# Another order of the sixteen attention units, with the decay table's squares on ScalarE and the first unit's own-key products on GpSimd

## Chip, cores and metric

The kernel runs on one core of a Trainium2 chip. The metric is the device time of one execution in microseconds (us), as the median of several runs; lower is better. Each program was also run once under the hardware profiler, and the rows quoted here come from that execution.

## What is computed

Three blocks follow one another. Cut to what matters:

```python
# attention, batch 4, 8 heads, 768 tokens, head size 48: a decaying state per head
for t in range(S):
    cur = u * k[t] v[t]^T
    y[t] = r[t] (state + cur)
    state = w * state + k[t] v[t]^T
# soft mixture of experts: 3072 tokens x 384, 8 experts with 4 slots each, inner size 1024
logits = x @ phi
d = softmax(logits, over tokens)
slot_input = d.T @ x
slot_out[e] = relu(slot_input[e] @ w1[e]) @ w2[e]
y = softmax(logits, over slots) @ slot_out
# feed-forward: 384 -> 2048 -> 384
out = relu(y @ w_in) ** 2 @ w_out
```

## The kernel before

**Units.** The attention's work is cut into sixteen units, one for each of 4 batches and 4 pairs of heads, in this order. A unit has 768 tokens, taken as six chunks of 128. Its inputs arrive by one group of loads (`load_unit`, L93 and L97) in one of five unit buffers. `decay` (L236, VectorE) multiplies keys and receptances by powers of the decay w from a table. `turns` (L263 to L276) does two transposes on TensorE: the keys of a coming unit, and the attention output of an earlier unit into `xn`, with the copies on ScalarE. `A` (L306) makes the products of keys and receptances inside a chunk, `KV` (L318) the chunk states, `scan` (L322, VectorE) runs the states through the chunks, `cp` (L311, VectorE) copies the masked products, `inter` (L336) and `intra` (L345, copies L348) add up the output: the part from the state and the part inside the chunk. `pr1`, `pr2`, `weigh` and `diag` (L280 to L295) make the term of a token's own key on GpSimd and VectorE. For units 0 to 2 that term is made in another way: `rk` (L491) multiplies keys and receptances elementwise, `dg_of` (L498) sums them on TensorE.

**The decay table.** `base` holds w. L207 to L216 build the table on VectorE: a copy of w, five squares (L209), the reciprocals of all six powers in one instruction (L210), and six products (L216) that double the filled part of the table each time. TensorE meanwhile does warm-up products (`keep_clock`, L227) and fillers (`filler`, L231), whose results nobody reads.

**The soft mixture.** `L` (L371) adds a unit's logits; when the four units of a batch (a block) are through, `soft1a` to `soft1d` take maxima and exponentials, `both` (L408) transposes them, and `soft3` (L463) multiplies them with the block's attention output. That output is `xn`, of which there are two: blocks 0 and 2 use `xn[0]`, blocks 1 and 3 `xn[1]`. `xn[0]` is a part of the big buffer of slot 13 (`sh0`; the names slot_14 in the order's rows are its). `soft4` (L473) adds a block's sums to the totals P2. Of the last block the sums are formed in the lines behind the attention. After it come the experts' first product (`up`, L998) and second (`down`, L1018), the token sums of the experts' output (L1114, with a copy of the middle third on VectorE, L1115), the products of these with w_in (`G`, L1123), and the feed-forward proper, which is TensorE's work to the end (L1166, L1275).

**Loads.** All loads are issued by SyncE (SP) in the order in which they stand in the program, and each waits there until its buffer is free. Besides the units these are the first product's weights w1 in 24 pieces (`load_piece`, L196), the second's, w2, as whole experts (`load_weight` 8 to 15, L193), four quarters of w_in (`load_win`, L149) and sixteen pieces of w_out (`load_wout`, L177). The weights go where a unit's buffer has become free; the first quarter of w_in goes into slot 13, once `xn[0]` has been read for the last time. w_in and w_out hold 8-byte numbers, of which VectorE makes 4-byte ones (L156, L158, L160, three instructions for a piece).

**Order.** The order of instructions on each engine is that of the calls in the program, written out by hand (`tc.manual_schedule()`); the list of calls from `decay(0, 1, EV)` on is what the change rewrites. Each tile's tag and number of buffers sets which earlier use a write waits for.

Of the kernel before, what the change touches and what calls it, by code (L numbers as in the profile page):

```python
# [9 lines left out]
F32R = mybir.dt.float32r  # L10
# [7 lines left out]
def rwkv_softmoe_ffn(ctx: ExitStack, tc: tile.TileContext, un, wt, ph, w1, w2, w_in, w_out, out):  # L18
# [119 lines left out]
    nc.scalar.activation(warm[:, 0:1], warm[:, 1:2], AF.Exp)  # L138
# [90 lines left out]
    def filler(n):  # L229
        for _ in range(n):  # L230
            nc.tensor.matmul(pp[:, 384:512], ident, ident, start=True, stop=True)  # L231

# [250 lines left out]
    keep_clock(6)  # L483
# [62 lines left out]

    decay(0, 1, EV)
    load_piece(10)
    decay(0, 1, OD)
    carry_of()  # L550
    decay(0, 0, EV)
    rk(0, EV)
    decay(0, 0, OD)
    rk(0, OD, nc.vector)
    filler(2)
    turns(None, 0)
    A(0, 0)
    decay(1, 1)
    A(0, 1)
# [3 lines left out]
    filler(2)  # L563
    rsc_of()
    filler(2)
    decay(1, 0)
    filler(2)
    filler(2)
    scan(0)
    cp(0, 1)  # L570
    turns(None, 1)
    ones_of()
    filler(2)
    UT_of()
    diag(0, 0)
    cp(0, 0)
    inter(0)
    rk(1)
    dg_of(1)
    diag(1, 1)  # L580
    intra(0, 0)
    KV(1)
    decay(2, 0)
    decay(2, 1)
    rk(2)
    intra(0, 1)
# [24 lines left out]
    decay(4, 0)
    L(0)
    A(2, 1)
    cp(2, 0)
    inter(2)
    intra(2, 0)
    diag(2, 1)
    cp(2, 1)
    pr2(3)
    decay(4, 1)  # L620
    pr1(4)
    load_piece(5)
    KV(3)
    weigh(3)
    diag(3, 0)
    diag(3, 1)
    scan(3)
    intra(2, 1)
    pr1(5)
    A(3, 0)  # L630
    turns(1, 4)
    decay(5, 1)
    L(1)
    cp(3, 0)
    load_piece(8)
    pr2(4)
    A(3, 1)
    turns(2, 5)
    load_unit(7)
    decay(6, 0)  # L640
    cp(3, 1)
    L(2)
    decay(5, 0)
    A(4, 0)
    inter(3)
    KV(4)
    weigh(4)
    diag(4, 0)
    decay(6, 1)
    scan(4)  # L650
    cp(4, 0)
    load_piece(3)
    intra(3, 0)
    intra(3, 1)
    A(4, 1)
    turns(3, 6)
    L(3)
    soft1d(0)
    pr2(5)
    weigh(5)  # L660
    diag(4, 1)
    A(5, 0)
    cp(4, 1)
    load_piece(15)
    diag(5, 0)
    pr1(6)
    decay(7, 1)
    cp(5, 0)
    pr2(6)
    load_unit(8)  # L670
    soft1a(0)
    soft1b(0)
    load_piece(4)
    inter(4)
    diag(5, 1)
    decay(7, 0)
    KV(5)
    scan(5)
    intra(4, 0)
    intra(4, 1)  # L680
    load_unit(9)
    A(5, 1)
    cp(5, 1)
    turns(4, 7)
    load_piece(17)
    pr1(7)
    weigh(6)
    decay(8, 0)
    both(0)
    c_max(0)  # L690
    A(6, 0)
    inter(5)
    intra(5, 0)
    diag(6, 0)
    cp(6, 0)
    KV(6)
    c_sub(0)
    diag(6, 1)
    load_piece(14)
    pr2(7)  # L700
    intra(5, 1)
    load_unit(10)
    decay(8, 1)
    A(6, 1)
    load_piece(2)
    turns(5, 8)
    load_piece(6)
    pr1(8)
    L(4)
    L(5)  # L710
    cp(6, 1)
    weigh(7)
    scan(6)
    pr1(9)
    soft3(0)
    decay(9, 1)
    diag(7, 0)
    A(7, 0)
    inter(6)
    cp(7, 0)  # L720
    load_piece(23)
    intra(6, 0)
    KV(7)
    intra(6, 1)
    load_unit(11)
    pr2(8)
    scan(7)
    diag(7, 1)
    A(7, 1)
    turns(6, 9)  # L730
    L(6)
    weigh(8)
    A(8, 0)
    diag(8, 0)
    inter(7)
    intra(7, 0)
    cp(7, 1)
    decay(10, 1)
    pr2(9)
    diag(8, 1)  # L740
    soft1c(0)
    KV(8)
    cp(8, 0)
    decay(9, 0)
    scan(8)
    c_exp(0)
    intra(7, 1)
    decay(10, 0)
    c_sum(0)
    A(8, 1)  # L750
    cp(8, 1)
    weigh(9)
    load_piece(16)
    turns(7, 10)
    load_piece(0)
    L(7)
    A(9, 0)
    soft1a(1)
    inter(8)
    soft1b(1)  # L760
    KV(9)
    load_unit(12)
    decay(11, 1)
    load_piece(18)
    intra(8, 0)
    intra(8, 1)
    scan(9)
    KV(10)
    pr1(10)
    pr2(10)  # L770
    load_piece(11)
    diag(9, 0)
    A(9, 1)
    diag(9, 1)
    cp(9, 0)
    load_unit(13)
    turns(8, 11)
    both(1)
    cp(9, 1)
    A(10, 0)  # L780
    inter(9)
    pr1(11)
    weigh(10)
    diag(10, 0)
    intra(9, 0)
    diag(10, 1)
    scan(10)
    KV(11)
    soft1c(1)
    intra(9, 1)  # L790
    A(10, 1)
    c_max(1)
    load_piece(12)
    load_unit(14)
    decay(12, 1)
    load_piece(21)
    cp(10, 0)
    turns(9, 12)
    decay(11, 0)
    pr2(11)  # L800
    L(8)
    pr1(12)
    cp(10, 1)
    L(9)
    A(11, 0)
    scan(11)
    inter(10)
    load_piece(22)
# [540 lines left out]
```

## Time and profile before

| what | value |
|---|---|
| median of 3 runs | 370.85 us (370.64 to 371.09) |
| the profiled execution | 370.69 us, span 369.0 us |
| TensorE products busy | 362.9 us, 98% |
| VectorE busy | 266.8 us, 72% |
| ScalarE busy | 203.6 us, 55% |
| GpSimd busy | 101.8 us, 28% |

The span is the time from the first to the last instruction in the trace. The parts of the kernel lie in it like this: the head to about 16 us, the attention to about 111 us, the experts' first product from 116.5 to 127.7 us, their second from 129.0 to 139.5 us, the first feed-forward product at 141.25 us, and the feed-forward to the end. Busy shares are means over the span; what the rows in the section below show are single stretches.

### The profile page before, as it was taken

To read this page: it belongs to the slowest core of one execution; us is meant where nothing else is said; L and a number is where in the kernel's file an instruction comes from. 1 tells how busy PE (TensorE), PEld (TensorE's weight loads), DVE (VectorE), ACT (ScalarE), POOL (GpSimd) and SP (SyncE) were. 2 spreads that over 40 slices of the span, in tenths; PEclk is the share of its full clock that TensorE was granted. 3 is DMA by queue.
4 is the path that set the end of the run, shared out by engine and by line. 5 is a ranking of instruction groups with operands and counts; after the bars stand their busy time and mean duration, and the time that the engine had idled before them with its cause. 6 is when DMAs were issued, how large, how long until landed. Compare 5 with 4: busy or idle time off the path is not lost.

```text
span 369.0 us, 9048 instructions
## 1 busy us (share of the span) xinstructions
PE 362.9 (98%) x3694; PEld 295.0 (80%) x3694; DVE 266.8 (72%) x457; ACT 203.6 (55%) x441; POOL 101.8 (28%) x119
## 2 busy tenths in 40 slices
PE   7999999999999999999999999999999999999996
PEld 6888888897986637787878888888888888888884
DVE  7879878889675687999876676666666766666663
ACT  3244444544444217987878765555555755555553
POOL 4558886686744112222222400000000000000000
PEclk9999999999999999999999999999999999999999
DMA  7999899999999998333422022000000210000004
GB/s 247 411 366 412 298 376 388 405 376 408 351 360 410 419 417 333 95 110 93 108 92 68 2 85 85 3 0 0 2 1 0 114 60 0 2 1 0 0 2 171
DMA packets 22665, 65.22 MB, mean 177 GB/s; under 512 B 2544, under 2 KB 4832, under 8 KB 22624
## 3 DMA queue, kind: packets, MB, share of 16 engines
q1 hardware_dynamic: 22624, 64.65, 46.5%
q8 instruction: 29, 0.48, 0.5%
q14 instruction: 12, 0.10, 0.1%
HBM read 59.00 MB, written 4.72 MB: 173 GB/s over the span
## 4 chain that ended last, share of the span: by engine, by line
PE 97%; DVE 1%; DMA 1%; ACT 0%; issue 0%
PE ps_A L1275 26%; PE ps_tab L1275 9%; PE ps_kv L1275 9%; PE ps_lg L1275 9%; PE ps_A L306 7%; PE ps_YO L336 3%; PE ps_YE L345 3%; PE ps_YO L1166 3%; PE ps_YE L1166 3%; PE ps_A L998 3%; PE ps_YO L345 3%; PE ps_tab L1018 3%; PE ps_lg L371 2%; PE ps_kv L318 2%; PE ps_YE L269 2%; PE ps_kv L269 1%
## 5 line engine op out<-in xcount | busy, mean ns | idle before, releaser
L1190 DVE TENSOR_TENSOR slot<-slot,slot 128x512 fp32r<-128x512 f32 (+1 forms) x97 | 70.2, 725 | 55.1 <-PE ps_A L1275 18.6
L1275 PE MATMUL ps_A<-slot,slot 128*128 128x512 f32 x429 | 105.1, 389 | 0.0
L1275 PEld LDWEIGHTS ps_A<-slot,slot 128*128 128x128 f32 x429 | 80.5, 188 | 16.7
L1187 ACT CAST slot<-slot 128x512 fp32r<-128x512 f32 x95 | 59.1, 622 | 49.0 <-DVE slot L1184 48.7
L1275 PE MATMUL ps_tab<-slot,slot 128*128 128x512 f32 x144 | 55.5, 392 | 0.0
L1184 DVE TENSOR_TENSOR slot<-slot 128x512 f32<-128x512 f32 x68 | 47.0, 691 | 11.4 <-ACT slot L1177 11.2
L1275 PE MATMUL ps_kv<-slot,slot 128*128 128x512 f32 x144 | 55.1, 389 | 0.0
L1275 PE MATMUL ps_lg<-slot,slot 128*128 128x512 f32 x144 | 55.0, 389 | 0.0
L311 DVE COPY_PREDICATED AT<-mask,ps_A 128x384 f32<-128x384 int32 x63 | 33.5, 584 | 7.6 <-PE ps_A L306 3.2
L1177 ACT ACTIVATE slot<-ps_YO 128x512 f32<-128x512 f32 (+1 forms) x49 | 28.8, 590 | 12.1 <-PE ps_YO L1166 11.5
L1177 ACT ACTIVATE slot<-ps_YE 128x512 f32<-128x512 f32 x48 | 28.8, 599 | 12.1 <-PE ps_YE L1166 11.8
L295 POOL TENSOR_SCALAR_AFFINE_SELECT AT<-dg 128x768 f32<-128x768 f32 x32 | 28.1, 883 | 20.0 <-DVE dg L288 7.4
L1049 POOL TENSOR_TENSOR slot<-wf,slot 128x384 fp32r<-128x384 f32 x16 | 17.3, 1082 | 58.9 <-ACT slot L1044 58.9
L1275 PEld LDWEIGHTS ps_tab<-slot,slot 128*128 128x128 f32 x144 | 27.0, 188 | 6.0 <-issue 0.6
L1275 PEld LDWEIGHTS ps_kv<-slot,slot 128*128 128x128 f32 x144 | 27.0, 188 | 5.7
L1275 PEld LDWEIGHTS ps_lg<-slot,slot 128*128 128x128 f32 x144 | 27.0, 188 | 5.5
L306 PE MATMUL ps_A<-slot 48*128 48x128 f32 x378 | 30.3, 288 | 0.0
L236 DVE TENSOR_TENSOR slot<-slot,ps_tab 112x768 f32<-112x768 f32 (+1 forms) x34 | 29.8, 889 | 0.0
L306 PEld LDWEIGHTS ps_A<-slot 48*128 48x128 f32 x378 | 24.5, 187 | 4.9 <-issue 3.2
L348 ACT COPY xT<-ps_YE 112x384 f32<-112x384 f32 x16 | 7.7, 481 | 23.4 <-PE ps_YE L345 23.4
L284 POOL TENSOR_TENSOR slot<-slot,slot 128x576 f32<-128x576 f32 x13 | 18.5, 1419 | 7.6 <-ACT slot L276 7.5
L1166 PE MATMUL ps_YO<-slot,slot 128*128 128x512 f32 x48 | 18.9, 393 | 0.0
(233 smaller groups left out, 562.0 us busy)
## 6 DMA issues: line engine op xcount, KB each, us to landing
slot<-in_un_dram SPq DMA_DIRECT2D x12, 1344.0 KB, 7.8
slot<-in_w_dram SPq DMA_DIRECT2D x24, 512.0 KB, 9.2
slot<-in_w_dram SPq DMA_DIRECT2D x8, 1536.0 KB, 10.0
slot<-in_w_in_dram SPq DMA_DIRECT2D x4, 1536.0 KB, 10.5
wo<-in_w_out_dram SPq DMA_DIRECT2D x16, 384.0 KB, 3.3
out_dram<-slot SPq DMA_DIRECT2D x18, 256.0 KB, 2.1
slot<-in_un_dram SPq DMA_DIRECT2D x9, 448.0 KB, 6.6
slot<-slot SPq DMA_DIRECT2D x56, 16.0 KB, 1.9
```

Source lines behind the costliest of these rows:

```text
L236: nc.vector.tensor_tensor(x, x, t.unsqueeze(1).to_broadcast(list(x.shape)), ALU.mult)
L284: nc.gpsimd.tensor_tensor(rv, rv, st[n, "kn"] if by is None else by, ALU.mult)
L295: nc.gpsimd.affine_select(out=at, in_=dg.unsqueeze(3).to_broadcast([128, 2, HC, 128]), pattern=[[0, 2], [0, HC], [1, 128]], compare_op=ALU ...
L306: nc.tensor.matmul(p[h][:, i], tv[rows, 1, 2 * i + par], tv[rows, 0, 2 * i + par], start=True, stop=True)
L311: nc.vector.copy_predicated(st[n, "AT", par][:, h], mask.unsqueeze(1).to_broadcast([128, HC, 128]), p)
L345: nc.tensor.matmul(p[o:o + D, i], vv[:, 2 * i + par, h], at[:, h, i], start=False, stop=True, skip_group_check=True)
L1166: nc.tensor.matmul(p, gst[:, 128 * f:128 * (f + 1)], cTall[:, 512 * g:512 * (g + 1)], start=True, stop=True)
L1177: nc.scalar.activation(fs[i, "hr"][:, c], fs[i, "p"][:, c], AF.Relu)
L1184: nc.vector.tensor_mul(gg, hr, hr)
L1187: nc.scalar.copy(part(i, "gh")[:, c], fs[i, "gg"][:, c])
L1190: nc.vector.tensor_tensor(part(i, "gl")[:, c], fs[i, "gg"][:, c], fs[i, "gh"].bitcast(F32)[:, c], ALU.subtract)
L1275: nc.tensor.matmul(o, (hi, lo, hi)[k][:, 128 * j:128 * (j + 1)], (gh, gh, gl)[k], start=(f == 0 and k == 0 and i > 0), stop=(f == NF - 1 a ...
```

## The change

Five things change in the head: the five squares of the table go from VectorE to ScalarE (as activations of the kind Square, with the early exponential of L138 behind them), the copy of w goes to GpSimd, the one reciprocal of all powers becomes three that stand between the products, two of the six warm-up products go, and both halves of unit 0's own-key products are on GpSimd (one half of unit 1's is now on VectorE). A function `idle` is added that nothing calls. Behind that the list of calls is another: the same units in the same order with the same instructions, interleaved in another way, and with the loads at other places between them. Cut to what is spoken of:

```diff
-    nc.scalar.activation(warm[:, 0:1], warm[:, 1:2], AF.Exp)
...
-    nc.vector.tensor_copy(pos[:, 0], base[:, :NP])
     for i in range(5):
-        nc.vector.tensor_mul(pos[:, i + 1], pos[:, i], pos[:, i])
-    nc.vector.reciprocal(neg[:, :6], pos[:, :6])
-    nc.vector.tensor_copy(tabp[:, :, 63:64], neg[:, 0].unsqueeze(2))
+        nc.scalar.activation(pos[:, i + 1], pos[:, i] if i else base[:, :NP], AF.Square)
+    nc.scalar.activation(warm[:, 0:1], warm[:, 1:2], AF.Exp)
+    nc.gpsimd.tensor_copy(pos[:, 0], base[:, :NP])
     for i in range(6):
         n = 1 << i
+        if i == 0:
+            nc.vector.reciprocal(neg[:, 0], base[:, :NP])
+            nc.vector.tensor_copy(tabp[:, :, 63:64], neg[:, 0].unsqueeze(2))
+        elif i in (1, 3):
+            nc.vector.reciprocal(neg[:, i:3 * i // 2 + 2], pos[:, i:3 * i // 2 + 2])
...
-    keep_clock(6)
+    keep_clock(4)
...
-    rk(0, OD, nc.vector)
+    rk(0, OD)
...
-    soft3(2)
-    inter(14)
...
     turns(14, None)
     c_max(2)
     c_sub(2)
+    soft3(2)
+    inter(15)
```

In the rows of the order an engine's instructions stand in sequence; `xN` is a count of like ones in a row. VectorE in the head, before, from the table's first row on; slot_14_84 is slot 13's buffer with the powers of w, ps_tab the table, slot_1_71 unit 0:

```order
L207 COPY slot_14_84<-base 112x4
L209 TENSOR_TENSOR slot_14_84<-slot_14_84 112x4 x5
L210 RECIPROCAL slot_14_84<-slot_14_84 112x24
L211 COPY ps_tab_122<-slot_14_84 112x4
L216 TENSOR_TENSOR ps_tab_122<-ps_tab_122,slot_14_84 112x4x2
...
L236 TENSOR_TENSOR slot_1_71<-slot_1_71,ps_tab_122 112x3x128 x4
L491 TENSOR_TENSOR slot_1_71<-slot_1_71 112x3x128
```

And now:

```order
L213 RECIPROCAL slot_14_84<-base 112x4
L214 COPY ps_tab_121<-slot_14_84 112x4
L219 TENSOR_TENSOR ps_tab_121<-ps_tab_121,slot_14_84 112x4x2
L216 RECIPROCAL slot_14_84<-slot_14_84 112x8
L219 TENSOR_TENSOR ps_tab_121<-ps_tab_121,slot_14_84 112x4x2x2
L219 TENSOR_TENSOR ps_tab_121<-ps_tab_121,slot_14_84 112x4x2x4
L216 RECIPROCAL slot_14_84<-slot_14_84 112x12
...
L244 TENSOR_TENSOR slot_1_71<-slot_1_71,ps_tab_121 112x3x128 x4
L511 TENSOR_TENSOR slot_13_83<-ps_tab_121,slot_14_84 112x512
```

The squares (L209) and the own-key half (L491) are gone from this engine; the reciprocals are three and stand between the products.

TensorE at the end of the attention, before; slot_5_75 is unit 14's buffer, slot_1_71 unit 15's, and L463 reads slot 13's:

```order
L371 MATMUL ps_lg_1867<-xT_1708,phs 32x128 x6
L463 MATMUL ps_A_1876<-slot_14_84,nat_1777 32x385 x6
L336 MATMUL ps_YO_117<-slot_5_75,slot_15_85 48x128 x2
...
L345 MATMUL ps_YE_116<-AT_1790,slot_5_75 48x128 x6
L345 MATMUL ps_YO_117<-AT_1874,slot_5_75 48x128 x6
L318 MATMUL ps_kv_115<-slot_1_71,slot_15_85 48x48 x10
...
L269 MATMUL ps_YE_116<-ident,xT_1909 128x48
...
L371 MATMUL ps_lg_1867<-xT_1808,phs 32x128 x6
L371 MATMUL ps_lg_1867<-xT_1909,phs 32x128 x6
L336 MATMUL ps_YO_117<-slot_1_71,slot_15_85 48x128 x2
```

And now, where L379, L344, L353, L326, L277 and L471 are the lines L371, L336, L345, L318, L269 and L463 of before:

```order
L379 MATMUL ps_lg_1871<-xT_1831,phs 32x128 x6
...
L344 MATMUL ps_YO_116<-slot_5_75,slot_15_85 48x128 x2
...
L326 MATMUL ps_kv_114<-slot_1_71,slot_15_85 48x48 x10
L353 MATMUL ps_YE_115<-AT_1792,slot_5_75 48x128 x6
L353 MATMUL ps_YO_116<-AT_1852,slot_5_75 48x128 x6
...
L277 MATMUL ps_YO_116<-ident,xT_1930 128x48
L471 MATMUL ps_A_1970<-slot_14_84,nat_1799 32x385 x6
L344 MATMUL ps_YO_116<-slot_1_71,slot_15_85 48x128 x2
...
L353 MATMUL ps_YE_115<-AT_1892,slot_1_71 48x128 x6
L353 MATMUL ps_YO_116<-AT_1894,slot_1_71 48x128 x6
L379 MATMUL ps_lg_1871<-xT_1930,phs 32x128 x6
```

The slot sums of block 2 (L463, now L471) have moved from ahead of unit 14's inter products to ahead of unit 15's, and one logits group from ahead of unit 15's inter products to behind its intra products.

SP's queue behind them, now (w2 of expert 2, the first quarter of w_in into slot 13, w2 of experts 3, 4 and 5, the second quarter, the last two of w2, and w_out):

```order
L192 DMA slot_154_1750<-in_w_dram 128x3x1024
L148 DMA slot_155_1752<-in_w_in_dram 128x3x1024
L192 DMA slot_156_1754<-in_w_dram 128x3x1024
L192 DMA slot_164_1813<-in_w_dram 128x3x1024
L192 DMA slot_167_1842<-in_w_dram 128x3x1024
L148 DMA slot_214_2145<-in_w_in_dram 128x3x1024
L192 DMA slot_215_2159<-in_w_dram 128x3x1024
L192 DMA slot_216_2173<-in_w_dram 128x3x1024
L176 DMA wo_2175<-in_w_out_dram 128x768
```

Kinds and sizes are those of before, and the loads behind the first quarter of w_in still stand behind it; only experts 4 and 5 have changed places.

## Rows read from the trace of the kernel before

**Rows 1.** The page: busy line; moved bytes in 40 slices of 9.2 us; chain

```profile
PE 362.9 (98%) x3694; PEld 295.0 (80%) x3694; DVE 266.8 (72%) x457; ACT 203.6 (55%) x441; POOL 101.8 (28%) x119
...
DVE  7879878889675687999876676666666766666663
...
GB/s 247 411 366 412 298 376 388 405 376 408 351 360 410 419 417 333 95 110 93 108 92 68 2 85 85 3 0 0 2 1 0 114 60 0 2 1 0 0 2 171
...
PE 97%; DVE 1%; DMA 1%; ACT 0%; issue 0%
```

**Rows 2.** TensorE's waits (us, times, longest); 20 to 110 us: busy us of each engine

```profile
PE ps_lg L227 <- POOL ident masks.py:199: 1.4, 1, 1.4
PE ps_kv L498 <- issue: 0.2, 1, 0.2
...
20.00:110.00 90.00, 89.96 (x1878) 77.64 (x1879) 74.46 (x127) 42.07 (x135) 63.88 (x63) 1.00 0.98 374
```

**Rows 3.** Timeline of VectorE in the head: start, us, engine, line, operation

```profile
2.90 0.97 DVE L209 TENSOR_TENSOR slot<-slot 112x4 f32<-112x4 f32 x5
3.90 0.30 DVE L210 RECIPROCAL slot<-slot 112x24 f32<-112x24 f32 x1
...
4.44 1.69 DVE L216 TENSOR_TENSOR ps_tab<-ps_tab,slot 112x8 f32<-112x8 f32 x6
...
6.17 1.95 DVE L236 TENSOR_TENSOR slot<-slot,ps_tab 112x384 f32<-112x384 f32 x4
...
8.15 0.99 DVE L491 TENSOR_TENSOR slot<-slot 112x384 f32<-112x384 f32 x1
```

**Rows 4.** Timeline of TensorE, ScalarE and GpSimd in the head

```profile
1.43 4.81 PE L227 MATMUL ps_lg<-ident 128*128 128x256 f32 x12 [1.43 <-POOL ident masks.py:199]
...
2.31 0.20 ACT L138 ACTIVATE warm<-warm 1x1 f32<-1x1 f32 x1 [0.22 <-POOL warm L137]
...
6.08 0.61 PE L231 MATMUL ps_lg<-ident 128*128 128x128 f32 x4
...
7.73 1.00 POOL L491 TENSOR_TENSOR slot<-slot 112x384 f32<-112x384 f32 x1 [3.23 <-DVE slot L236]
```

**Rows 5.** SP's waits: waiter, what for, us in all, times, longest

```profile
SPq L149 <- PE ps_A L463: 3.2, 1, 3.2
```

**Rows 6.** The chain of waits: start, us, engine, tile, line, count

```profile
101.97 1.30 PE ps_A L463 x12
...
108.08 1.00 PE ps_lg L371 x24
...
129.04 10.46 PE ps_tab L1018 x128
...
141.25 0.67 PE ps_tab L1123 x6
```

**Rows 7.** Timeline of SP's queue, where loads are issued: start of the issue, its length

```profile
94.52 0.38 SPq L193 DMA_DIRECT2D slot<-in_w_dram  x1
...
99.78 0.37 SPq L193 DMA_DIRECT2D slot<-in_w_dram  x1
...
103.46 0.37 SPq L149 DMA_DIRECT2D slot<-in_w_in_dram  x1
```

**Rows 8.** DMA issues at 94.5, 99.8, 103.5, 1.3 us (us to landing); 98 to 116 us in 40

```profile
slot<-in_w_dram SPq DMA_DIRECT2D x1, 1536.0 KB, 8.1
...
slot<-in_w_dram SPq DMA_DIRECT2D x1, 1536.0 KB, 8.8
...
slot<-in_w_in_dram SPq DMA_DIRECT2D x1, 1536.0 KB, 8.9
...
slot<-in_un_dram SPq DMA_DIRECT2D x1, 448.0 KB, 3.6
...
GB/s 419 346 382 391 419 291 218 146 91 237 328 391 373 391 391 428 364 273 328 419 428 410 401 428 419 428 382 364 373 382 401 355 400 419 410 410 419 419 419 419
```

**Rows 9.** Timeline of VectorE where w_out lands

```profile
136.86 0.36 DVE L156 TENSOR_SCALAR wf<-wo 128x384 int32<-128x384 int32 x1 [1.06 <-DMA wo<-in_w_out_dram]
...
140.63 0.29 DVE L1115 COPY slot<-ps_A 128x128 f32<-128x128 f32 x1
```

More of the change, by code (lines that the diff above doesn't have):

```diff
@@ L231, in filler, with idle @@
             nc.tensor.matmul(pp[:, 384:512], ident, ident, start=True, stop=True)
+    def idle(n, m, cols):
+        p = ps("A")
+        for _ in range(n):
+            nc.tensor.matmul(p[:m, :cols], ident[:, :m], ident[:, :cols], start=True, stop=True)
     def decay(n, m, cols=slice(0, NC)):
@@ L646, in rwkv_softmoe_ffn @@
     KV(4)
+    pr2(4)
+    decay(5, 0)
+    load_unit(7)
+    load_piece(3)
+    load_piece(15)
+    cp(3, 1)
     weigh(4)
@@ L649, in rwkv_softmoe_ffn @@
     decay(6, 1)
-    scan(4)
[L651 to L655, printed above, removed]
+    pr1(5)
+    decay(6, 0)
+    intra(3, 0)
+    diag(4, 1)
+    intra(3, 1)
+    cp(4, 0)
+    A(4, 1)
+    pr2(5)
+    scan(4)
+    cp(4, 1)
+    weigh(5)
+    decay(7, 0)
+    decay(7, 1)
     turns(3, 6)
     L(3)
[L658 to L661, printed above, removed]
+    soft1a(0)
+    diag(5, 0)
     A(5, 0)
-    cp(4, 1)
-    load_piece(15)
-    diag(5, 0)
+    inter(4)
+    intra(4, 0)
@@ L666, in rwkv_softmoe_ffn @@
     pr1(6)
-    decay(7, 1)
+    diag(5, 1)
+    load_unit(8)
+    load_piece(4)
     cp(5, 0)
     pr2(6)
-    load_unit(8)
-    soft1a(0)
+    KV(5)
+    intra(4, 1)
+    scan(5)
     soft1b(0)
[L673 to L681, printed above, removed]
     A(5, 1)
-    cp(5, 1)
     turns(4, 7)
[L685 to L688, printed above, removed]
     both(0)
-    c_max(0)
     A(6, 0)
     inter(5)
+    cp(5, 1)
@@ L693, in rwkv_softmoe_ffn @@
+    constants()
     intra(5, 0)
-    diag(6, 0)
-    cp(6, 0)
[L696 to L708, printed above, removed]
-    L(4)
-    L(5)
+    pr1(7)
+    KV(6)
+    weigh(6)
+    load_unit(9)
+    load_piece(17)
+    load_piece(14)
+    intra(5, 1)
+    diag(6, 0)
+    decay(8, 1)
+    pr2(7)
+    A(6, 1)
+    pr1(8)
+    turns(5, 8)
+    cp(6, 0)
@@ L711, in rwkv_softmoe_ffn @@
+    weigh(7)
+    L(4)
+    L(5)
+    ones_of()
+    decay(8, 0)
+    load_unit(10)
+    load_piece(2)
+    load_piece(6)
+    load_piece(23)
+    diag(6, 1)
     cp(6, 1)
-    weigh(7)
+    soft3(0)
     scan(6)
[L714 to L717, printed above, removed]
     A(7, 0)
     inter(6)
+    decay(9, 0)
+    diag(7, 0)
+    pr1(9)
     cp(7, 0)
-    load_piece(23)
     intra(6, 0)
+    c_max(0)
+    decay(9, 1)
     KV(7)
+    scan(7)
     intra(6, 1)
-    load_unit(11)
+    A(7, 1)
@@ L751, in rwkv_softmoe_ffn @@
[L751 to L759, printed above, removed]
-    soft1b(1)
[L761 to L772, printed above, removed]
+    turns(7, 10)
+    weigh(9)
+    load_unit(11)
+    load_piece(16)
+    load_piece(0)
+    soft1d(0)
+    diag(8, 1)
+    decay(10, 0)
+    L(7)
+    cp(8, 1)
@@ L773, in rwkv_softmoe_ffn @@
+    soft1a(1)
+    A(9, 0)
+    decay(11, 1)
+    diag(9, 0)
+    inter(8)
+    c_sub(0)
+    KV(9)
+    intra(8, 0)
+    scan(9)
+    load_unit(12)
+    load_piece(18)
+    load_piece(11)
+    intra(8, 1)
+    pr1(10)
+    KV(10)
+    pr1(11)
+    cp(9, 0)
+    load_unit(13)
+    load_piece(12)
+    c_exp(0)
+    soft1b(1)
     A(9, 1)
     diag(9, 1)
-    cp(9, 0)
-    load_unit(13)
+    soft1c(1)
     turns(8, 11)
+    cp(9, 1)
+    pr2(10)
+    weigh(10)
+    diag(10, 0)
     both(1)
-    cp(9, 1)
@@ L852, in rwkv_softmoe_ffn @@
-    load_weight(9)
-    soft1a(2)
-    A(13, 0)
-    inter(12)
-    intra(12, 0)
-    pr1(14)
-    intra(12, 1)
-    soft1c(2)
-    scan(13)
-    load_weight(10)
-    A(13, 1)
-    diag(13, 0)
-    decay(15, 1)
-    soft1b(2)
-    pr2(14)
-    turns(12, 15)
+    c_max(1)
+    decay(13, 0)
+    scan(12)
+    c_sum(0)
+    pr2(12)
+    weigh(12)
+    L(10)
+    inter(11)
+    intra(11, 0)
+    intra(11, 1)
+    decay(14, 1)
+    pr2(13)
+    load_weight(8)
+    weigh(13)
+    diag(12, 0)
+    KV(13)
@@ L868, in rwkv_softmoe_ffn @@
+    diag(12, 1)
+    A(12, 1)
+    cp(12, 1)
+    turns(11, 14)
+    A(12, 0)
+    cp(12, 0)
+    L(11)
+    soft1a(2)
+    diag(13, 0)
+    c_div(0)
+    inter(12)
+    pr1(14)
+    c_sub(1)
+    scan(13)
+    A(13, 0)
+    pr1(15)
+    decay(14, 0)
     diag(13, 1)
     cp(13, 0)
+    c_exp(1)
+    load_weight(9)
+    intra(12, 0)
+    KV(14)
+    intra(12, 1)
+    A(13, 1)
+    decay(15, 1)
+    cp(13, 1)
+    load_weight(10)
+    load_win(0, take(NSLOT, I32))
+    load_weight(11)
+    soft1b(2)
```

254 lines of the change are left out of this document (105 added, 149 removed).

## The prediction

> **What bounds the kernel now.** I read the page's busy line and its chain first. TensorE is busy 98% of the span and makes up 97% of the chain that ended last; VectorE and ScalarE stay at 72% and 55% [rows 1]. Then the waits of TensorE alone: the longest is 1.4 us, for the identity at the very start, the next is 0.2, and from 20 to 110 us it is busy 89.96 of 90.00 us [rows 2]. So the sixteen units run on TensorE without a gap, and another order of them has nothing to win there. What can still move are the head, before TensorE is continuous, and whatever TensorE's order releases elsewhere. For the second I read the moved bytes: from about 10 us to 138 us the DMA engines carry some 300 to 420 GB/s, and 410 to 419 in the slices from 110 to 138 us, which is all they reach anywhere [rows 1]. From 85 us on this one queue brings nothing but weights, and the rows of VectorE near 137 us show that the first pieces of w_out, the last of that stream, are used on landing [rows 9]. The kernel has two bounds of nearly equal length, then: TensorE, and the weight stream.
>
> **The change, part by part.** *The decay table.* Between the landing of the base and the first decay VectorE now does five squares (0.97 us), one reciprocal (0.30), a copy and six products (1.69); the first decay starts at 6.17 [rows 3]. The change takes the squares and the copy before them (taken as long as a square, 0.2) off VectorE, 1.2 us, and puts three reciprocals where one was. Each of the two added ones costs between 0.2, what a square of this size takes, and the 0.30 of the present one. Left over are 0.6 to 0.8 us; I take 0.65. ScalarE's five squares run beside it: the smallest ACTIVATE shown took 0.20 [rows 4], five take 1.0 to 1.5 us, and VectorE asks for the last of them only after two reciprocals, a copy and three products, some 1.5 us in. So they are hidden or cost 0.1 to 0.2 us; if that cover goes, the table is where it was.
>
> *The head on GpSimd and TensorE.* Half of the own-key products leaves VectorE (0.99 us [rows 3]) for GpSimd, which needs 1.00 for such a half [rows 4]. GpSimd can begin once three of the four decays (1.95 us together [rows 3]) are done, at 6.17 - 0.65 + 1.46 = 7.0, and does two in a row, done at 9.0, where VectorE ended its half at 9.1: nothing for TensorE's products that wait for both, 1 us of room on VectorE. What queues behind them on GpSimd, the diagonal masks, needs those products anyway. Two of the six warm-up products go; all six took from 1.43 to 6.08, in twelve passes [rows 4], but TensorE waits for the table in any case, so that is worth nothing. The twelve filler products stay; the new filler function is called nowhere. TensorE thus gets its unit work earlier by 0 (ScalarE late) to 0.8 (all of it arrives): I take **0.5 us**.
>
> *The units' order.* Each decay, product, scan and copy is still issued, on the same engine, 0.5 us earlier. Loads are grouped differently, unit loads before the weight pieces, but the number and sizes are the same, and the queue is full either way. Those cost nothing as long as TensorE has no wait in 20 to 110 us; VectorE is busy 74.46 of 90.00 us there [rows 2], so half a us either way is taken up.
>
> *The third block's slot sums (soft3 of block 2).* This is the move that I cost most. It reads the attention output in the big buffer of slot 13. The first quarter of w_in is loaded into that same buffer, so its load waits for the last of these products. The trace shows the wait: SP's queue stood 3.2 us for TensorE's L463 [rows 5], which ended at 101.97 + 1.30 = 103.27 [rows 6], and the load left at 103.46 [rows 7]. SP issues in order, so behind this load stand all later weights: w2 of experts 3, 5 and 4, another quarter of w_in, the last two w2 and the first pieces of w_out. In the new order these products come after the last but one transpose block, with only the last unit's inter and intra products and two logits groups still to come. In the present trace that unit's inter products follow two logits groups that take 1.00 us from 108.08 on [rows 6]; both now stand elsewhere, one before and one behind. The work ahead of the inter products is else the same, so the moved products end where the inter products begin, 109.08, less the 0.50 of the group that went behind and the head's 0.50: 108.08. With SP's 0.2 us from release to issue, as now, the load leaves at **108.3** instead of 103.46. ScalarE's scaled copy of these sums and VectorE's update of the totals move with them; their reader is the last block's sum, and a whole unit's output and two logits groups lie between: nothing.
>
> What does 4.8 us of delay cost? Before, the queue was not empty from this load on: the transfer ahead, issued at 99.78, landed 8.8 us later at 108.6, and the quarter of w_in landed 8.9 us after its issue, at 112.4 [rows 7, 8]. Now it finds a drained queue. The nearest rows are two transfers of 1536 KB that were issued 5.3 us apart, at 94.52 and 99.78 [rows 7]: they took 8.1 and 8.8 us, and the moved bytes around the second, in slices of 0.45 us, fall from 400 to 91 GB/s some 2 us after its issue and are back a us later [rows 8]. So that queue had nearly run dry too, and a dry queue costs the 2 us before the first bytes as well as the bytes. I take the quicker one: 108.3 + 8.1 = 116.4, **4.0 us later**. The other end is the very first 448 KB load on an idle queue, 3.6 us [rows 8]; its other 1088 KB at 410 GB/s [rows 1] add 2.7, so 6.3 us, and 2.2 us later. The upper end is 8.8: 4.7 later. Everything behind follows at the same pace, because that stretch already runs at the top rate.
>
> The Trainium skill's page DMA: Bandwidth & Descriptors, section Anatomy of one DMA, gives about 2.0 us plus bytes over 436 GB/s for one transfer, for transfers issued from GpSimd; an estimate from it is 5.6 us for 1536 KB, a shift of 1.5 us and a time of 371.7. The trace disagrees for transfers of this size on SP's queue, with 8.1 and 8.8 us.
>
> Who waits for the stream? VectorE idles 1.06 us for w_out and starts on it at 136.86, the moment it lands; 3.77 us later, at 140.63, comes its copy of the middle third of the token sums, 0.29 long [rows 9]. The first feed-forward product needs that copy and starts at 141.25 for 0.67 us [rows 6]. With w_out 4.0 later the copy ends at 144.92; two thirds of the product (0.45) come after it, so it ends at 145.4 instead of 141.92: **+3.5 us**. The last w2, just ahead of w_out in the queue (384 KB at 410 GB/s is 1.0 us), lands near 139.9 and its eighth of the 10.46 us of expert products [rows 6] ends by 141.2, which is earlier, so TensorE stands twice for over 2 us but the copy decides. The head's 0.5 us is contained: it only brings the late load forward. After that TensorE is the bound again, nothing is there to regain, and the rest shifts as a whole.
>
> Sum, against the profiled execution's own 370.69 us (span 369.0, 1.7 around it; the median of the runs is 370.85, 0.16 above): 370.69 + 3.5 = **374.2 us**. With the bounds of the landing (+1.7 and +4.2) and of the head (0 to 0.8 instead of 0.5): 372.1 to 375.4.
>
> **Rivals.** *The clock falls in the new gaps.* TensorE would idle some 2 us before the last expert and 2 us before the first feed-forward product, longer than anywhere now. At the start, where it had done nothing, twelve passes of 256 columns took 4.65 us from start to start, while the four of 128 columns behind them took 0.61 [rows 4]: by that pace the twelve should take 24/4 times as much, 3.7, at most, so the lower level (1.2 of 2.4 GHz) cost between 1.0 and half of 4.65. Take 2: 376.2. For it: TensorE stands twice within some 5 us. Against it: the work between the gaps. The Trainium skill's page TensorE: Matmul & The Clock Gate, Part 1, states that idleness throttles and activity releases; no run here shows a gap of this length.
>
> *The queue restarts quickly.* If a drained queue behaves as at the program's start (6.3 us), the shift is 2.2 - 0.5 = 1.7: 372.4. For it: then no engine lags behind another. Against it: the two 1536 KB transfers, one of which met an all but dry queue.
>
> *Faster.* The place is the head: table, squares and the freed VectorE could bring the whole attention forward. Each us there moves the w_in load forward by the same us, so this decides only from 4.0 us on, when the stream has no hole left; 0.75 more gives 370.0. Against it: VectorE's head holds 3.3 us of table work in all, and TensorE never waits later. That ScalarE's squares are no quicker than VectorE's (the change not doing what it says) adds 0.5 instead: 374.7.
>
> **How the numbers follow.** 0.2% is 0.74 us, about what a measurement of this kernel can tell. Late w_in load without a clock loss (372.1 to 375.4, likeliest 374.2): 0.67. With a clock loss (375.2 to 377.5): 0.14. Quick restart (371.6 to 372.8): 0.08. Quick restart and a head worth 1.5 us more, no measurable change: 0.06. Faster: 0.05. Slower is 0.89. The range from 372.0 to 376.6 leaves out the last two cases, part of the quick restart and the worse half of the clock case, under 0.2 in all.
>
> **What would show it.** After: the w_in load of slot 13 leaves near 108.3, behind L471; moved bytes dip for some 4 us around 108 to 111; w_out lands near 140.8; VectorE's copy into the token sums starts near 144.6; TensorE waits before the last expert and before the first feed-forward product; first decay near 5.5. Wrong, if that load leaves before 105, if w_out lands by 137.3, or if TensorE shows no wait between 135 and 146.

## The result and the profile after

| | before | changed |
|---|---|---|
| median of 4 runs | 370.97 us (370.64 to 372.71) | 375.53 us (374.63 to 376.83) |
| ratio to before | | 1.012, 95% interval 1.0088 to 1.0152 |
| profiled execution | 370.69 us, span 369.0 | 375.96 us, span 374.2 |
| mean granted clock of TensorE | 1.0 | 0.995 |

The changed kernel is 1.2% slower. Single executions over 1.5% longer than the fastest of their kernel are left out of the ratios below, and kept in the medians. Its page (in the order of [rows 1]: busy line, granted clock and moved bytes in 40 slices of 9.4 us, chain by engine):

```profile
PE 364.8 (97%) x3690; PEld 295.8 (79%) x3690; DVE 266.0 (71%) x453; ACT 203.8 (54%) x446; POOL 101.7 (27%) x121
...
PEclk9989999999999999999999999999999999999999
...
GB/s 247 411 278 412 353 353 386 410 368 374 379 187 383 419 418 420 184 106 96 101 98 63 7 10 160 2 1 0 2 1 0 84 87 0 0 3 0 0 2 168
...
PE 89%; DMA 6%; issue 1%; ACT 1%; DVE 1%; POOL 1%; SPq 0%; POOLq 0%
```

Busy times are nearly those of before (TensorE 1.9 us more). What is new: 6% of the chain is a DMA, the moved bytes fall to 187 GB/s in the slice from 103 to 112 us (360 before), and the clock dips in the third slice. SP's queue, to be held against [rows 5, 7, 8]: its wait for the slot sums, the issue of w_in's first quarter, its landing time, and the moved bytes from 106 to 124 us in slices of 0.45 us:

```profile
SPq L148 <- PE ps_A L471: 8.1, 1, 8.1
...
102.54 0.37 SPq L192 DMA_DIRECT2D slot<-in_w_dram  x1
111.13 0.37 SPq L148 DMA_DIRECT2D slot<-in_w_in_dram  x1
...
slot<-in_w_in_dram SPq DMA_DIRECT2D x1, 1536.0 KB, 6.3
...
GB/s 419 428 464 373 391 155 36 18 0 0 55 0 0 64 127 191 328 346 400 391 410 437 428 410 428 428 428 400 419 400 428 464 373 419 410 419 419 410 428 400
```

The load waits 8.1 us instead of 3.2, leaves at 111.13 instead of 103.46 and lands 6.3 us later, at 117.4 instead of 112.4. From 108.3 to about 112.8, for some 4.5 us, the DMA engines move 155 GB/s at most and mostly far less; they are at full rate from 114 on. What waits at the other end (VectorE and ScalarE where w_out lands, to be held against [rows 9]; then TensorE's waits):

```profile
142.25 0.36 DVE L155 TENSOR_SCALAR wf<-wo 128x384 int32<-128x384 int32 x1 [3.08 <-DMA wo<-in_w_out_dram]
...
145.86 0.28 DVE L1124 COPY slot<-ps_A 128x128 f32<-128x128 f32 x1
...
143.83 0.51 ACT L1053 CAST slot<-wf 128x384 fp32r<-128x384 f32 x1 [11.42 <-DVE wf L159]
144.25 0.59 ACT L1119 COPY slot<-ps_tab 128x128 f32<-128x128 f32 x3
...
PE ps_A L1123 <- ACT slot L1119: 1.2, 1, 1.2
PE ps_A L314 <- DVE slot L244: 0.8, 1, 0.8
PE ps_tab L1027 <- DMA slot<-in_w_dram: 0.8, 1, 0.8
```

w_out lands at 142.25 (136.86 before) and VectorE's copy comes at 145.86 (140.63), 5.2 us later; the span is 5.2 us longer. ScalarE is a second link that the prediction did not name: its copy of the first converted piece (L1053) waits for VectorE, and the copies of the experts' output that TensorE's token sums need (L1119) stand behind it. TensorE waits 0.8 us for the last expert's weights and 1.2 us for those copies.

The head did what was forecast up to one point (VectorE's decays, GpSimd's own-key products):

```profile
5.00 1.02 DVE L244 TENSOR_TENSOR slot<-slot,ps_tab 112x384 f32<-112x384 f32 x2
6.40 1.02 DVE L244 TENSOR_TENSOR slot<-slot,ps_tab 112x384 f32<-112x384 f32 x2 [0.38 <-DMA slot<-in_un_dram]
...
7.03 1.97 POOL L499 TENSOR_TENSOR slot<-slot 112x384 f32<-112x384 f32 x2 [2.77 <-DVE slot L244]
```

The table is there at 5.0 us (6.17 before, [rows 3]), but the second pair of decays waits for unit 0's third load and starts at 6.40. TensorE's first unit product waits for it: the 0.8 us in its waits above.

And one thing was not forecast at all. TensorE's clock falls in the head (busy us in stretches of 2 us in the order PE, PEld, DVE, ACT, POOL, then the granted clock, the DMA share and GB/s):

```profile
20.00:22.00 2.00, 1.59 (x64) 1.23 (x65) 1.07 (x2) 0.10 (x1) 0.80 (x1) 1.00 1.00 404
22.00:24.00 2.00, 2.00 (x48) 1.98 (x49) 0.00 (x0) 0.52 (x2) 1.12 (x2) 0.58 1.03 422
24.00:26.00 2.00, 2.00 (x30) 1.64 (x28) 1.47 (x2) 0.39 (x2) 0.62 (x1) 0.57 0.30 116
```

Means of 0.58 and 0.57 say that for most of these 4 us TensorE ran at the lower of its two levels, 1.2 of 2.4 GHz. Ahead of it it was busy 1.59 of 2 us, with unit 2's own-key sums (L506) and a gap of 0.41 us among them. In the new gaps at 140 to 146 us, where the prediction looked for it, the clock stayed at 1.00.

### The profile page after: what moved, and what is told of

Read it like the earlier page. It is cut to its first block, busy times and chain, and to the rows that moved or that the text cites. A ratio compares the mean times of both kernels' runs of the same rounds, so it can differ in the third digit from the quotient of the medians.

```text
span 374.2 us, 9032 instructions
## 1 busy us (share of the span) xinstructions
PE 364.8 (97%) x3690; PEld 295.8 (79%) x3690; DVE 266.0 (71%) x453; ACT 203.8 (54%) x446; POOL 101.7 (27%) x121
## 4 chain that ended last, share of the span: by engine, by line
PE 89%; DMA 6%; issue 1%; ACT 1%; DVE 1%; POOL 1%; SPq 0%; POOLq 0%
PE ps_A L1284 26%; PE ps_tab L1284 9%; PE ps_kv L1284 9%; PE ps_lg L1284 9%; PE ps_A L314 7%; DMA wo<-in_w_out_dram 5%; PE ps_YE L353 3%; PE ps_YO L344 3%; PE ps_YO L1175 3%; PE ps_YO L353 3%; PE ps_YE L1175 3%; PE ps_lg L379 2%; PE ps_kv L326 2%; PE ps_YE L277 2%; PE ps_A L1007 1%; DMA slot<-in_un_dram 1%
## 5 line engine op out<-in xcount | busy, mean ns | idle before, releaser
L1199 DVE TENSOR_TENSOR slot<-slot,slot 128x512 fp32r<-128x512 f32 (+1 forms) x97 | 71.4, 737 | 55.3 <-PE ps_kv L1284 18.5
L1284 PE MATMUL ps_A<-slot,slot 128*128 128x512 f32 x429 | 105.1, 389 | 0.0
L1284 PEld LDWEIGHTS ps_A<-slot,slot 128*128 128x128 f32 x429 | 80.5, 188 | 16.7
L1284 PE MATMUL ps_tab<-slot,slot 128*128 128x512 f32 x144 | 55.5, 392 | 0.0
L1284 PE MATMUL ps_kv<-slot,slot 128*128 128x512 f32 x144 | 55.1, 389 | 0.0
L1284 PE MATMUL ps_lg<-slot,slot 128*128 128x512 f32 x144 | 55.0, 389 | 0.0
L314 PE MATMUL ps_A<-slot 48*128 48x128 f32 x378 | 31.1, 289 | 0.8 <-DVE slot L244 0.8
L1284 PEld LDWEIGHTS ps_tab<-slot,slot 128*128 128x128 f32 x144 | 27.0, 188 | 6.1 <-issue 0.6
L1284 PEld LDWEIGHTS ps_kv<-slot,slot 128*128 128x128 f32 x144 | 27.0, 188 | 5.7
L1284 PEld LDWEIGHTS ps_lg<-slot,slot 128*128 128x128 f32 x144 | 27.0, 188 | 5.5
L1175 PE MATMUL ps_YO<-slot,slot 128*128 128x512 f32 x48 | 18.9, 393 | 0.3 <-ACT slot L1186 0.3
```

The source lines that it names most:

```text
L314: nc.tensor.matmul(p[h][:, i], tv[rows, 1, 2 * i + par], tv[rows, 0, 2 * i + par], start=True, stop=True)
L1175: nc.tensor.matmul(p, gst[:, 128 * f:128 * (f + 1)], cTall[:, 512 * g:512 * (g + 1)], start=True, stop=True)
L1199: nc.vector.tensor_tensor(part(i, "gl")[:, c], fs[i, "gg"][:, c], fs[i, "gh"].bitcast(F32)[:, c], ALU.subtract)
L1284: nc.tensor.matmul(o, (hi, lo, hi)[k][:, 128 * j:128 * (j + 1)], (gh, gh, gl)[k], start=(f == 0 and k == 0 and i > 0), stop=(f == NF - 1 a ...
```

## The experiments

Two theories. A: the late w_in load sets the end, by SP standing in front of it. B: that load is covered, and the loss is the clock and the new order. Each experiment ran beside the kernel before on the same chip: the time in front of "against" is the median of the experiment, the one behind it that of the kernel before.

**1. The sums put back in the changed kernel.**

```diff
     soft4(1)
     soft1c(2)
+    soft1d(2)
+    soft3(2)
     inter(14)
...
     intra(14, 1)
-    soft1d(2)
...
     c_sub(2)
-    soft3(2)
     inter(15)
```

> The changed kernel with one thing undone: the slot sums of block 2 (and the small factors they need) stand ahead of unit 14's inter products again. Theory A (the late w_in load sets the end): the load leaves near 106 instead of 111.1, the moved bytes have no hole, w_out lands by 138.5 instead of 142.25, and the time falls by about 3 us, to 373.0 if TensorE's clock falls in the attention as in the profiled execution (its products then start 2.3 us late at the experts), or to 370.9 if it does not. Theory B (the late load is covered, the loss is TensorE's clock and the new order): the time stays within 1 us of the changed kernel's 375.5.

373.12 us against 371.06, ratio 1.0055 (1.0025 to 1.0085). The load left at 106.42, and w_out landed at 140.2:

```profile
106.42 0.37 SPq L148 DMA_DIRECT2D slot<-in_w_in_dram  x1
...
140.19 0.36 DVE L155 TENSOR_SCALAR wf<-wo 128x384 int32<-128x384 int32 x1 [1.84 <-DMA wo<-in_w_out_dram]
```

Some 2.5 of the 4.6 us are gone, as theory A has it, but 2.1 stay. Two reasons show in its profile. The clock fell from 22 to 26 us here too, and in 4 of 12 executions the mean is below 0.996; the 8 others have a median of 372.84. And the edit has a price of its own: without the sums between the last transposes and unit 15's inter products, TensorE waits there for ScalarE's copies:

```profile
PE ps_YO L344 <- ACT xn L280: 0.9, 1, 0.9
```

**2. The sums moved alone, in the kernel before.**

```diff
-    soft3(2)
     inter(14)
...
     soft4(1)
-    soft4(2)
...
     turns(14, None)
+    soft3(2)
...
     inter(15)
+    soft4(2)
```

> The kernel before with one thing changed: the slot sums of block 2 stand behind the last but one transpose block, as in the change. Theory A: the w_in load leaves near 108.3. If a dry queue needs 6.3 us for it, as in the changed kernel's profile, w_out lands 2.2 us later and the time is 372.4 (+1.7); if it needs 8.1, as forecast, 374.2 (+3.5). Theory B (no cost of its own): 370.8, within 0.4 us of before.

374.67 us against 371.06, ratio 1.0087 (1.0053 to 1.0120); 7 runs, none with a mean clock below 0.998. This one move (with the update of the totals that follows it) makes +3.6 us of the change's +4.6, without a fallen clock and without anything else of the change. That the late load is covered, as theory B has it, is out. The profile repeats the whole chain:

```profile
SPq L149 <- PE ps_A L463: 8.6, 1, 8.6
...
110.70 0.37 SPq L149 DMA_DIRECT2D slot<-in_w_in_dram  x1
...
slot<-in_w_in_dram SPq DMA_DIRECT2D x1, 1536.0 KB, 6.6
...
142.25 0.36 DVE L156 TENSOR_SCALAR wf<-wo 128x384 int32<-128x384 int32 x1 [3.53 <-DMA wo<-in_w_out_dram]
145.85 0.28 DVE L1115 COPY slot<-ps_A 128x128 f32<-128x128 f32 x1
```

The load needed 6.6 us, not 8.1, and still the time is that of the dear estimate, because the load left later than the 108.3 expected. In this execution, the longest of the seven, TensorE was 1.8 us late by the first block's sums, among others with two waits that end by nothing the trace shows ("issue", 0.8 and 0.7 us); from 10 to 24 us the DMA engines moved 356 to 379 GB/s, against 403 to 425 in the execution of before.

**3. Four fillers ahead of unit 2's own-key sums,** in the changed kernel.

```diff
     pr1(3)
+    filler(4)
     dg_of(2)
```

> The changed kernel with four filler products ahead of unit 2's own-key sums on TensorE, where the clock fell in the profiled execution just behind. Theory C (TensorE's thin work and short gap at 21 to 22 us let the clock fall): granted clock 1.0 throughout, TensorE's attention ends 1.5 us earlier (2.1 won, 0.6 for the fillers), the w_in load leaves near 109.6 and the time is about 374.4 in nearly every run. Theory D (the clock falls for what lies earlier, the idle 0.8 us at 6 to 7 us or the fewer warm-up products): it still falls, and the time is that of the changed kernel or 0.6 more.

376.08 us against 371.06, ratio 1.0126 (1.0084 to 1.0168). The clock held (0.998 to 1.0 in all 6 runs), as theory C has it. Six runs alone could be chance; over all experiments the mean clock was below 0.997 in 2 of 40 executions with the fillers and in 23 of 61 without. The idle 0.8 us at 6 to 7 us, theory D's candidate, is not enough to bring the clock down: the profile of experiment 9 has 0.9 us there and the full clock. But the time did not fall. In the profiled execution TensorE lost time elsewhere in the first 30 us (busy 1.66 of 2 us at 16 to 18 and 1.80 at 28 to 30), and the w_in load left at 110.91, 0.2 us ahead of the changed kernel's. As a gain the fillers are a miss, and why they did not pay here stays open.

**4. Both, sums back and fillers.**

> The changed kernel with both: the slot sums of block 2 back ahead of unit 14's inter products, and four fillers ahead of unit 2's own-key sums. If what is left over before in the run with the sums back (373.1 against 371.1) is the fallen clock, the clock stays at 1.0 here, TensorE starts the experts 1.5 us earlier than there (117.5 instead of 119.0), the weights of experts 1 and 2 leave earlier too, and the time is 371.5 or less. If it is the order itself (unit loads that are asked for later, other waits in the first 30 us), the time stays near 373 though the clock holds.

372.87 us against 370.77, ratio 1.0054 (1.0031 to 1.0077). No run below 0.999, and the granted clock of the stretch in which it fell is whole:

```profile
20.00:22.00 2.00, 2.00 (x30) 1.65 (x28) 1.06 (x2) 0.00 (x0) 0.66 (x1) 1.00 1.01 408
22.00:24.00 2.00, 2.00 (x87) 1.97 (x88) 0.04 (x1) 0.66 (x2) 1.01 (x2) 1.00 1.02 417
24.00:26.00 2.00, 2.00 (x46) 1.80 (x42) 2.00 (x4) 0.72 (x2) 0.68 (x1) 1.00 0.65 157
```

TensorE started the experts at 118.5 instead of the 117.5 expected, 2.1 later than before, and w_out landed at 139.1, 2.3 later than before; the 0.9 us wait of experiment 1 was there again. The clock is not what is left over.

**5. The decay table alone,** in the kernel before (the diff of the table, as shown with the change).

> The kernel before with the change's decay table alone (squares on ScalarE, copy on GpSimd, three reciprocals); the order of units, the own-key products and the warm-up products stay. Theory A says that the end hangs on the weight stream: the first decay starts 0.7 to 1.2 us earlier if unit 0's loads have landed, TensorE's attention ends up to 0.5 earlier, and the time stays within 0.3 us of before (370.5 to 371.1). Rival: TensorE sets the end, and the time falls by the 0.5 (370.3). Rival 2: the earlier start only meets the loads of unit 0, which landed near 6.4 in the changed kernel, and TensorE gains nothing.

371.34 us against 371.06, ratio 1.0006 (0.9974 to 1.0038): no difference that shows. The first decay started at 5.16 and TensorE was 0.6 us ahead by unit 2's key transposes (18.3 against 18.9), but 0.5 behind by unit 6's (39.5 against 39.0), with an "issue" wait of 0.8 us between. A late start of an engine that is busy to the end should count in full; in this execution it was lost to other waits, so whether the 0.6 us are worth anything stays open.

**6. The conversions of w_out behind the token sums,** in the changed kernel. The loop over the first two pieces (six VectorE instructions, two copies of the high parts, two subtractions) goes from ahead of `down(6)` to ahead of `wout_f32(2, 0)`.

> The changed kernel with VectorE's conversions of the first two pieces of w_out (and the copies of them on ScalarE and GpSimd) moved behind the copies of the token sums; the loads and TensorE's order stay. Theory A says that the first feed-forward product waits for w_out only because those conversions stand ahead on VectorE, and a copy of them ahead on ScalarE: then the token sums start right behind the last expert (ends near 142.7) and the first feed-forward product begins near 144.4 instead of 145.8, w_out still landing near 142.2, and the time falls by 1.0 to 1.5 us. If the products themselves need the converted pieces at once, the wait comes back behind them and the time stays within 0.4 us of the changed kernel's.

376.63 us against 370.77, ratio 1.0155 (1.0118 to 1.0192). The wait went and came back. TensorE around the first feed-forward products:

```profile
145.88 0.90 PE L1118 MATMUL ps_A<-sel,slot 128*128 128x128 f32 x6
...
147.05 0.83 PE L1132 MATMUL ps_tab<-slot,slot 128*128 128x128 f32 x6
149.42 0.86 PE L1147 MATMUL ps_lg<-slot,slot 128*32 128x128 f32 x24 [1.54 <-ACT slot L1033]
151.13 0.50 PE L1175 MATMUL ps_YO<-slot,slot 128*128 128x512 f32 x1 [0.85 <-DVE slot L1141]
```

w_out landed at 144.9 in this execution, in which TensorE was late as a whole. Counted from that landing, the first feed-forward product began 2.1 us behind it instead of 3.6 (145.8 and 142.2 in the changed kernel), as theory A says; but the next products waited 1.5 and 0.85 us, for a cast on ScalarE (L1033) and a product on VectorE (L1141) that now stood behind the conversions in the order of those engines, and the first main product (L1284) came 8.8 us behind the landing instead of 7.7. This order only moves the wait; that no order could dodge it is not shown.

**7. Only the place of the load in SP's queue,** in the changed kernel; the sums stay late.

```diff
     load_weight(10)
-    load_win(0, take(NSLOT, I32))
     load_weight(11)
+    load_win(0, take(NSLOT, I32))
```

> The changed kernel with one load moved: the first quarter of w_in is issued behind the second weights of expert 3, whose buffer comes free earlier, instead of ahead of them. The slot sums stay late. Theory A says that what costs is SP's queue standing still: then expert 3's weights leave near 107 and keep the DMA engines busy while w_in's quarter still leaves near 111; the hole in the moved bytes shrinks by some 2.5 us, w_out lands near 140 instead of 142.25, and the time falls by 1.5 to 2.5 us, to 373.0 to 374.0. If the place of the sums costs in another way (TensorE's or ScalarE's order), the time stays at 375.5.

372.16 us against 370.77, ratio 1.0039 (1.0018 to 1.0061): two lines exchanged leave 1.4 of the 4.6 us.

```profile
106.98 0.37 SPq L192 DMA_DIRECT2D slot<-in_w_dram  x1
...
109.67 0.37 SPq L148 DMA_DIRECT2D slot<-in_w_in_dram  x1
...
137.98 0.36 DVE L155 TENSOR_SCALAR wf<-wo 128x384 int32<-128x384 int32 x1 [1.24 <-DMA wo<-in_w_out_dram]
...
141.58 0.28 DVE L1124 COPY slot<-ps_A 128x128 f32<-128x128 f32 x1
```

The load itself still left late, at 109.67, but expert 3's weights went ahead of it at 106.98 into a buffer that was free, and w_out landed at 138.0. So it is not the late load that costs but the queue that stands behind it.

**8. The old table with the sums back,** the table's lines as before.

> The changed kernel with the slot sums of block 2 back, and the decay table as before: squares and one reciprocal on VectorE. The order of the units, the own-key products on GpSimd and the four warm-up products stay. The first decay starts near 6.2 instead of 5.0, but the second pair of decays waits for unit 0's third load, which lands near 6.4, either way: if the table is worth nothing, the time is that of the run with the sums back, 373.1 within 0.4. If the earlier table is worth the 0.5 us forecast, it is 0.5 longer; if the table on ScalarE is what costs the 2 us that are left, it falls to 371.1.

373.14 us against 370.77, ratio 1.0056 (1.0030 to 1.0082): as experiment 1, so in this order the new table is worth nothing that shows (the intervals are some 1 us to either side), and it is not what costs the rest.

**9. The change once more.**

> The changed kernel once more, on the same chip as the two below. Theory: the median stands near 375.5, some 4.5 above before; in a part of the executions the mean granted clock is below 0.996, and these are 1 to 2 us longer than the others. The w_in load leaves 7 us or more later than the 103.46 of before in the profiled execution, whether or not the clock falls there.

375.36 us against 370.71, ratio 1.0109 (1.0075 to 1.0143). Three runs at 1.0 have a median of 374.57, three at 0.994 and 0.995 one of 375.86: the fallen clock goes with 1.3 us here. The profiled execution is one of the first kind:

```profile
107.78 1.43 PE ps_A L471 x12
...
109.38 0.37 SPq L148 DMA_DIRECT2D slot<-in_w_in_dram  x1
...
slot<-in_w_in_dram SPq DMA_DIRECT2D x1, 1536.0 KB, 6.4
...
140.60 0.36 DVE L155 TENSOR_SCALAR wf<-wo 128x384 int32<-128x384 int32 x1 [3.10 <-DMA wo<-in_w_out_dram]
...
144.21 0.28 DVE L1124 COPY slot<-ps_A 128x128 f32<-128x128 f32 x1
...
22.00:24.00 2.00, 1.93 (x62) 1.91 (x63) 0.21 (x1) 0.66 (x2) 1.20 (x2) 1.00 1.02 419
```

**10. The sums back without that wait, with fillers.** `soft3(2)` behind `L(12)`, its factors a unit earlier, `L(13)` and `L(14)` behind the last transposes.

```diff
     cp(14, 0)
+    soft4(1)
+    soft1c(2)
...
     intra(13, 1)
+    soft1d(2)
...
     L(12)
-    L(13)
+    soft3(2)
...
     c_sub(2)
-    soft3(2)
+    L(13)
+    L(14)
     inter(15)
```

> The changed kernel with the slot sums of block 2 behind the logits of unit 12, where before had them, the small factors for them made a unit earlier, the logits of units 13 and 14 between the last transposes and unit 15's inter products (so that ScalarE's copies are covered, which cost TensorE 0.9 us in the first run with the sums back), and the four fillers. Theory: the w_in load leaves near 105, w_out lands by 138, TensorE has no wait over 0.5 us behind 30 us, the clock holds in all runs, and the time is 371.0 to 371.5, within 0.5 us of before: all that the change lost is then accounted for by the load's wait, the clock and that order. If something else in the new order costs, it stays at 372.5 or more.

371.73 us against 370.71, ratio 1.0017 (0.9995 to 1.0039); 11 of 12 runs lie between 371.4 and 373.0; the twelfth took 377.31 at a mean clock of 0.981, so the clock did not hold in all, as was expected. The load left at 104.85, w_out landed by 137.2, and VectorE's copy waits for TensorE again, not the other way round:

```profile
104.85 0.37 SPq L148 DMA_DIRECT2D slot<-in_w_in_dram  x1
...
137.17 0.36 DVE L155 TENSOR_SCALAR wf<-wo 128x384 int32<-128x384 int32 x1
...
142.09 0.29 DVE L1125 COPY slot<-ps_A 128x128 f32<-128x128 f32 x1 [1.23 <-PE ps_A L1124]
```

So the load's wait, the clock and that order together account for 3.6 of the 4.6 us; 1.0 stays, more than was expected, though the interval reaches down to no difference.

**11. Experiment 7 with the fillers.**

> The changed kernel with the load of w_in's first quarter behind expert 3's second weights (372.2 alone) and the four fillers. Theory: the fillers hold the clock near 22 us, so that no run has a mean clock below 0.997 (3 of 12 had without them), the slow runs of that version are gone, and the median is 371.8 or a little less; the 0.6 us of the fillers themselves is only paid where TensorE did not wait there anyway.

372.76 us against 370.71, ratio 1.0042 (1.0019 to 1.0065). The executions with a clock near 0.995 are gone, but one of the 12 took 378.23 at 0.980, and the median is not better than without the fillers: a miss on the time, and on the clock in that one execution.

**12. Experiment 10 without the fillers.**

> The version before last without its four fillers: the slot sums of block 2 where before had them, the logits of units 13 and 14 behind the last transposes. It splits the 1.0 us by which that version (371.73) stayed above before (370.71). If the fillers are what is paid, the executions with a mean clock over 0.997 take 371.1 or less and those in which the clock falls near 22 us 372.4 or more, some third of them. If the order itself costs the 1.0, the executions with the full clock stay at 371.7.

372.27 us against 370.60, ratio 1.0037 (1.0012 to 1.0062). The six executions with the full clock have a median of 371.5, six others lie between 372.1 and 377.2. So the fillers cost some 0.2 us in this order, not 0.6, and the order keeps most of the 1.0. In the profiled execution the clock fell earlier than in the changed kernel's, between 14 and 16 us (mean 0.77), and was at the lower level from 16 on, so it is not tied to one gap:

```profile
16.00:18.00 2.00, 2.00 (x66) 1.60 (x60) 1.99 (x3) 0.18 (x1) 0.30 (x1) 0.50 1.02 419
18.00:20.00 2.00, 2.00 (x34) 1.96 (x32) 0.25 (x1) 0.48 (x1) 1.60 (x3) 0.50 1.04 423
```

No version came out below the kernel before.

## Why the prediction held, point by point

**The bound and the move: right.** The end hangs on the weight stream as soon as SP stands still. The move that the prediction costed most makes +3.6 us alone (experiment 2), and letting expert 3's weights pass the waiting load gives 3.2 back (experiment 7). The chain was the one named: L471, the w_in load, w_out, VectorE's conversions, its copy into the token sums, the first feed-forward product.

**When the load leaves: 108.3 forecast, 109.38 and 111.13 found.** The sum took the head's 0.5 us as a gain that lasts. In the execution with the full clock TensorE was 0.3 us ahead at unit 2's key transposes (18.6 against 18.9), and 0.5 behind at those of unit 13's output (101.4 against 100.9): 1.0 us between forecast and trace. In the other execution the fallen clock is the main difference that its profile shows, and the load left 1.75 us later still.

**The dry queue: the step that failed.** The prediction took 8.1 us for the load, from two transfers that met a nearly dry queue, and gave 6.3 as the other end, worked out from the very first load [rows 8]. Found were 6.3 to 6.6, in all five profiles in which the DMA engines had stood nearly still before it (the change, experiments 2, 3, 6 and 9). After such a stand the load took what the prediction had worked out from the program's start; "quick restart" was right on the transfer and had 0.08 of the chances for its time. The two errors have opposite signs: 109.38 + 6.4 is 115.8, 0.6 before the forecast 116.4.

**From the load to the end.** "Everything behind follows at the same pace" was nearly so: w_out landed 3.7 us later in the execution with the full clock (140.60 against 136.86), the load itself 3.4. VectorE's copy came at 144.21 (forecast near 144.6), and this execution took 374.37 us against the 374.2 forecast. The number is good because the terms' errors cancel, not because each is.

**TensorE's gaps: smaller.** It waited 0.8 and 1.2 us (0.9 and 1.2 in experiment 9), where "over 2 us" each stood. The forecast had it half a us early at the last expert; it was late itself, as the experts began 2.3 us late in the first profile and 0.6 in the second. And the last weights were there at 139.6 in the second, not at 139.9.

**The clock: a rival with the wrong place.** Both profiles of the change read 1.00 in the new gaps; in the one in which the clock fell, it fell in the head, at 22 to 26 us. 5 of the change's 10 executions have a mean below 0.996 (where it fell in the others no trace shows), and in experiment 9 these took 1.3 us more than the rest. So the median of 375.53 lies 1.3 above the likeliest 374.2 and in the range that was given to this rival (375.2 to 377.5), but for a fall at another place. The rows that the prediction read for the clock were those of the program's start [rows 4], and it did not look behind them. Its price of 2 us came from the pace of the warm-up passes there, for which the trace has a granted clock of 1.00 (0 to 5 us): no row shows that the lower level made them slow.

**The head.** GpSimd's products ran from 7.03 to 9.00, as forecast (7.0 to 9.0), but by two errors that cancel. The decays began at 5.0 (5.5 forecast): from VectorE's first work on w to the first decay it took 2.52 us instead of 3.47, as the three reciprocals took 0.60 together (0.7 to 0.9 in the forecast), and w itself was there 0.2 us earlier in this execution (2.48 against 2.70), which is not the change's doing. What was missed is the load: the second pair of decays waits for unit 0's data, which land near 6.4 us.

**What stays open.** The prediction put the units' order at nothing, as TensorE had no wait from 20 to 110 us before. With the sums early and the clock full, the new order still costs 0.9 to 1.0 us (experiments 10 and 12); in the profile of experiment 10 TensorE begins the experts at 117.9 instead of 116.4. It was not taken apart further. Candidates that the traces show are waits of 0.3 to 1.5 us in the first 40 us, for VectorE, unit loads and nothing that the trace shows; none of them was tried alone.

## What to carry to other kernels

Where one queue issues all loads in order, the last reader of a buffer is a due time for everything behind the load that overwrites it: before moving such a reader later, look which load waits for it and what stands behind in that queue. If the reader must be late, let loads with free buffers pass (two lines exchanged were worth 3.2 us here). And a gain at an engine's start is a gain at the end only if no later wait takes it up: follow it from mark to mark before putting it into a sum.

## What was not expected of the hardware

The 1536 KB load of w_in's first quarter took 6.3 to 6.6 us on a queue that had stood nearly empty for some microseconds, 7.0 to 8.7 us where the transfer ahead was still ending (experiments 1, 4, 7, 8 and 10 to 12), and 8.9 in the kernel before. The page DMA: Bandwidth & Descriptors of the Trainium skill, section Anatomy of one DMA, gives about 2.0 us plus bytes over 436 GB/s for a transfer issued from GpSimd; the estimate from it was 5.6 us for this size, and SyncE's load on the nearly empty queue comes nearest to it, 0.7 to 1.0 us above.

The clock of the same program falls in some executions and not in others. With the change's order and no fillers, 23 of 61 executions had a mean clock below 0.997 (the changed kernel and experiments 1, 6, 7, 8, 9 and 12), with four fillers 2 of 40 (experiments 3, 4, 10 and 11), with the kernel before 6 of 88. The changed kernel's profile fell behind a stretch (20 to 22 us) with TensorE busy 1.59 of 2 us and a gap of 0.41; that of experiment 6 has the same 1.59 and the same gap there, and kept a clock of 1.00. Experiment 12's fell behind a stretch (12 to 14 us) with 0.73 of 2 us busy, and experiment 7's, with 0.89 there, did not. What decides between them was not found.
